# Moving a batched V group ahead of attention, and copying the first context in two halves

## The chip, the core and the metric

The kernel runs on one core of a Trainium2 chip. The metric is the device time of one execution in microseconds (us). The engines are TensorE (PE, with its weight loads as PEld), VectorE (DVE), ScalarE (ACT), GpSimd (POOL) and the DMA queues, the one of SyncE (SP) above all. PSUM, where matmuls leave their results, has eight banks; the text calls them by number.

## The reference

Two blocks follow each other. The first is attention with a recurrent memory: 2048 rows of 512 are cut into 64 segments of 32; in each, 8 memory rows are put ahead, and the first 8 output rows are the next segment's memory. So the segments are a chain.

```python
h = jnp.concatenate([mem, xs], axis=1)              # 8 + 32 rows
q, k, v = (jnp.einsum('btd,dhe->bhte', h, W) for W in (Wq, Wk, Wv))   # 32 heads of 128
scores = jnp.einsum('bhqe,bhke->bhqk', q, k) * scale
p = softmax(where(mask, scores, -1e9))
o = jnp.einsum('bhqk,bhke->bhqe', p, v)
o = jnp.einsum('bhte,hed->btd', o, Wo)
mem = o[:, :M, :]
outs.append(o[:, M:, :])
```

The second is a gMLP: `z = gelu(x @ w_in)`, the second half of z is normalised and mixed over all 2048 positions by `w_sp`, and the product with the first half goes through `w_out`. Both blocks have a layer norm ahead and a residual.

## The kernel before, in words

Every operation is recorded in program order with the tokens that it reads and writes; the recorder derives the semaphore waits, and each engine executes its own list in that order. There is no scheduler: the order of work is the order of the calls.

The loop over s runs through the 64 segments. A segment's 8 memory rows and 24 of its own rows form one stationary operand of 32 columns (`hT`); the last 8 rows of all segments of a chunk of 16 are computed in batches beforehand (`hTe`, "extra" rows). TensorE is used as four column tiles of 128x32 for the projections. The 32 heads are split into two halves b = 0, 1, and in each half into four c = 0 to 3 and four g = 0 to 3.

In a segment TensorE does, in this order: Q and K projections (`QK`, L533), scores (`S_half`, L584 and L590), the V projection (`V_half`, L639) with the softmax sums (`sm_sums`, L605 and L610) between its parts, one batched group of four steps popped from the list `gx`, then attention times V, then the output projection. The popped group is four times four matmuls: Q or K of a later chunk's extra rows (`qkx_mm`, L422) or their V (`vx_mm`, L472), and from segment 49 on part of the second block's first projection (`zp_mm`, L789). Segment 48 has none.

Attention times V is `PV_half(s, b)` for b = 0 and 1: 16 matmuls of 40 columns (L659) with K = 32, in four row tiles of 32x128, one for each c, and 4 matmuls (L666) for the extra rows. The four contexts c go into banks 6, 7, 0 and 1 (`PVB`), half b in columns 160 b to 160 b + 160. L659 of half b reads the normalised weights `E_sb` (DVE, L625) and V (`V_evac`, for b = 1 by DVE L651 and ACT L649), L666 reads the extra rows' weights (GpSimd, L629) and `Vx`, loaded by DMA. The last matmul of half 0's 16 also waits for both copies of half 1's V.

Behind it stands the list `gv`: further batched V groups (and, from segment 49, `zp_mm` groups) in bank 5 (`VXB`), cut into steps of four matmuls. `gv.pour(n)` issues up to n steps and stops when a group is complete, then returning its copy. Its n is `nC`: 3 in segments 0 to 3, 2 in each later segment with s % 4 = 1, else 1. From segment 4 on 8 (or 4, the others later) matmuls of the previous block of rows follow (`WoX_mm`, L738).

Then the four contexts are copied from PSUM to `cT`, each 128x320: c = 0 and 1 by ACT (L679), c = 2 and 3 by DVE (L681). The output projection `Wo` (L693) takes the contexts in the order 0, 2, 1, 3, eight matmuls of 256 columns each, first for output columns 0 to 256 in bank `OB` = 2, then for the rest in bank `OB2` = 0. ACT copies each half of the output into `part` (L705), a few small matmuls pick the memory rows (`mem_out`, L713), ACT puts them into the next segment's `hT` (L716), and the next segment's Q projection starts. Bank 2 also holds the V of half 1 and a piece of K; bank 6 also holds a piece of Q and softmax sums.

After the segments the second block runs, with its own loops.

Of the kernel before, what the change touches and what calls it, by code (L numbers as in the profile page):

```python
# [9 lines left out]
ACT = mybir.ActivationFunctionType  # L10
# [159 lines left out]
def fast_path(nc, st, keep, A_x, A_mem0, A_Wq, A_Wk, A_Wv, A_Wo, A_seg_len, B_w_in, B_w_sp, B_b_sp, B_w_out, out):  # L170
# [17 lines left out]
    scale = float(DH) ** -0.5  # L188
# [74 lines left out]
    ps = st.enter_context(nc.psum_tensor("f_ps", [128, 8, 512], F32))  # L263
# [5 lines left out]
    def PB(b):  # L269
        return ("ps", b)  # L270
# [147 lines left out]
    def qkx_mm(ck, mi, sg, b, bank, dc):  # L418
        ws = (w_q, w_k)[mi]
        for c in range(4):  # L420
            rhs = ws[:, dc, :].rearrange("p (h c i) -> p c h i", c=4, i=32)[:, c, 16 * b:16 * b + 16, :]
            pe(lambda e, c=c, rhs=rhs: e.matmul(ps[32 * c:32 * c + 32, bank, :], lhsT=hTe[:, ck, dc, 32 * sg:32 * sg + 32], rhs=rhs,  # L422
                                                start=(dc == 0), stop=(dc == DC - 1), tile_position=(0, 32 * c)),
               reads=[("hTe", ck), ("W", mi, 2 * b), ("W", mi, 2 * b + 1)], writes=[PB(bank)])

    def qkx_evac(ck, mi, sg, b, bank):
        tok = [("T", 0, 0), ("T", 0, 1)]
        act(lambda e: e.activation(out=Tst[:, 0, :].rearrange("p (hp i r) -> p hp i r", i=32, r=2),
                                   in_=ps[:, bank, :].rearrange("p (hp r i) -> p hp i r", r=2, i=32), func=ACT.Copy),
            reads=[PB(bank)], writes=tok)  # L430
        xi = Tst[:, 0, :].bitcast(U32)
        if mi == 0:
            xt = QTx[ck % 2][:, 0, sg, 8 * b:8 * b + 8, :, :].rearrange("p hp k r -> p (hp k r)").bitcast(U32)
        else:
            xt = KTu[ck % 2][:, 4 * b:4 * b + 4, :, 4 * sg:4 * sg + 4, :]
            xi = xi.rearrange("p (cb hp j k) -> p cb hp j k", j=4, hp=2, k=8)
        dve(lambda e: e.transpose(out=xt, in_=xi), reads=tok, writes=[("QTx", ck % 2, mi, sg, b)])
# [123 lines left out]
    def s_place(s, b):  # L561
        return SBK[b] if s == 0 or b else XB

# [80 lines left out]
    def V_evac(b, eng, gs=(0, 4), after=()):  # L644
# [5 lines left out]
        else:  # L650
            dve(lambda e: e.tensor_scalar(out=dst, in0=src, scalar1=VSC, scalar2=None, op0=ALU.mult), reads=[PB(bank)], writes=tok)  # L651

    def PV_half(s, b):
        xb = s % NVX
        for g in range(4):
            for c in range(4):
                q = slice(32 * c, 32 * c + 32)
                c0 = 160 * b + 40 * g
                pe(lambda e, q=q, c=c, g=g, c0=c0: e.matmul(  # L659
                    ps[:, PVB[c], c0:c0 + 40], lhsT=V_sb[q, b, g * 128:(g + 1) * 128], rhs=E_sb[q, b, 0:160].rearrange("p (a g t) -> p a g t", a=5, t=8)[:, :, g, :],  # L660
                    start=(g == 0), stop=False, skip_group_check=True, tile_position=(32 * c, 0)),
                    reads=[("V", b, g), ("E", b)], writes=[PB(PVB[c])],
                    after=[em.last_w[("V", 1, g)] for g in (0, 2)] if (b, g, c) == (0, 3, 3) else [])
        for c in range(4):
            q = slice(32 * c, 32 * c + 32)
            pe(lambda e, q=q, c=c: e.matmul(  # L666
                ps[:, PVB[c], 160 * b:160 * b + 160].rearrange("p (g q) -> p g q", q=40)[:, :, 0:16], lhsT=Vx[q, xb, b, :],
                rhs=E_sb[q, b, 160:224].rearrange("p (g q) -> p g q", q=16),
                start=False, stop=True, skip_group_check=True, tile_position=(32 * c, 0)),
                reads=[("Vx", xb), ("Ex", b)], writes=[PB(PVB[c])])  # L670

    UNSC = math.exp(-RBIAS)


    def cT_evac(c, eng):
        src = ps[:, PVB[c], 0:320]
        dst = cT[:, c, :]
        if eng == "act":
            act(lambda e: e.activation(out=dst, in_=src, func=ACT.Copy, scale=UNSC), reads=[PB(PVB[c])], writes=[("cT", c)])  # L679
        else:  # L680
            dve(lambda e: e.tensor_scalar(out=dst, in0=src, scalar1=UNSC, scalar2=None, op0=ALU.mult),  # L681
                reads=[PB(PVB[c])], writes=[("cT", c)])

    cTh = cT[:].rearrange("p c (b g q) -> p (c b g) q", b=2, q=40)


    def Wo(cs, bank, d0, d1):
        for c in cs:
            for bg in range(8):
                b, g = bg // 4, bg % 4  # L690
                h = 16 * b + 4 * c + g
                i = 8 * c + bg
                pe(lambda e, h=h, g=g, i=i, b=b, c=c: e.matmul(  # L693
                    ps[32 * g:32 * g + 32, bank, 0:d1 - d0], lhsT=cTh[:, i, 8:40], rhs=w_o[:, h, d0:d1], start=(c == 0 and b == 0),
                    stop=(c == 3 and b == 1), tile_position=(0, 32 * g)),
                    reads=[("cT", c), ("Wo", h // 8)], writes=[PB(bank)])

    def cTx_copy(s):
        j = s % 4
        dst = cTx[:, (s // 4) % 2, :, 8 * j:8 * j + 8]  # L700
        pool(lambda e: e.tensor_copy(out=dst, in_=cTh[:, :, 0:8]), reads=[("cT", c) for c in range(4)],
             writes=[("cTx", (s // 4) % 2)])

    def part_evac(s, bank, d0, d1):
# [29 lines left out]
    def WoX_mm(rb, qr, bgs=range(8)):  # L734
        for bg in bgs:
            b, g = bg // 4, bg % 4
            h = 16 * b + 4 * qr + g
            pe(lambda e, h=h, g=g, i=8 * qr + bg: e.matmul(ps[32 * g:32 * g + 32, WXB, :], lhsT=cTx[:, rb % 2, i, :], rhs=w_o[:, h, :],  # L738
                                                           start=(i < 4), stop=(i >= H - 4), tile_position=(0, 32 * g)),
               reads=[("cTx", rb % 2), ("Wo", h // 8)], writes=[PB(WXB)])  # L740
# [213 lines left out]
    def nC(s, rb, j4):  # L954
        if rb == 0:
            return 3
        return 2 if j4 == 1 else 1
# [9 lines left out]
    for s in range(NSEG):  # L967
        j4 = s % 4
        rb = s // 4
# [78 lines left out]
        xs = gx.pop(0) if gx else []  # L1048
        if s > 3 * CK and zcol:
            zr, zh = zcol.pop(0)  # L1050
            xs = [lambda dc=dc: zp_mm(zr, zh, XB, (dc,)) for dc in range(DC)] + [lambda: zp_evac(zr, zh, XB, "dve")]
        for f in xs[:4]:
            f()
        PV_half(s, 0)
        PV_half(s, 1)
        for f in xs[4:4]:
            f()
        late = []
        if s == 3 * CK + 1:
            for r, hf in zgap:  # L1060
# [13 lines left out]
        cT_evac(3, "dve")  # L1074
# [135 lines left out]
    def zbank():  # L1210
        zcnt[0] += 1
        return 5 + zcnt[0] % 3
# [26 lines left out]
    for i, rb in enumerate(order):  # L1239
# [3 lines left out]
        if i == 0:  # L1243
            F_group(RB - 1, XB)
            for qr in range(4):
# [10 lines left out]
        if i == 1:  # L1256
            WoX_scatter(RB - 1, XB)
            h_done(RB - 1, XB)
# [4 lines left out]
        if i in (3, 4):  # L1263
            r, j, bank = RB - 5 + i, i % 2, zbank()
# [822 lines left out]
```

## Time and profile before

| what | value |
|---|---|
| timed runs | 852.3, 853.75, 855.52 us; median 853.75 |
| the profiled execution's own time | 850.57 us |
| its span in the profile | 847.7 us |
| mean granted TensorE clock | 0.999 |
| the segments, from the first attention matmul of segment 0 to the last segment's | 50.5 to 681.8 us |

The profile shows one execution. A group's row has busy time and mean duration; in brackets, or behind the last bar, stands how long the engine had been idle and what released it. The timeline lists merged runs of equal instructions with their start and the time until the last of them ends. A matmul's duration contains its latency through the array, so matmuls that follow each other overlap in the rows; the chain of waits lists the pieces without this overlap, with the time from one to the next.

### The profile page before, as it was taken

The numbers are of one execution on the slowest core, as the hardware profiler recorded it, in microseconds if no ns is written. First come the engines' busy times: TensorE is split into PE (matmuls) and PEld (weight loads), VectorE is DVE, ScalarE is ACT, GpSimd is POOL, SyncE is SP. The second block draws the span as 40 slices with busy tenths as digits, with TensorE's granted clock in tenths as the row PEclk, the third lists the DMA queues.
The fourth block names the chain that finished last, engine by engine and source line by source line (L and its number), as shares of the span: only waits on it lengthen the run. The fifth ranks groups of instructions, "written<-read, shape, count | busy, mean of one in ns | idle before, by whom it ended". The sixth has DMA issues, their size and how long they took to land.

```text
span 847.7 us, 47962 instructions
## 1 busy us (share of the span) xinstructions
PE 833.5 (98%) x22028; PEld 486.8 (57%) x22034; DVE 493.5 (58%) x1175; ACT 494.0 (58%) x1355; POOL 155.1 (18%) x409
## 2 busy tenths in 40 slices
PE   8999999999999999999999999999999999999997
PEld 8666566656665565656655555556655644444443
DVE  4446566666665656665656666566656577553343
ACT  3456677676777777667777777666666676300000
POOL 5212111112211111121112111112211123100000
PEclk9999999999999999999999999999999999999999
DMA  9972222120201231232213021433332389033101
GB/s 330 385 225 78 70 46 62 51 78 20 82 29 44 63 73 42 66 56 53 69 38 79 30 77 52 83 76 71 70 84 57 71 276 298 1 99 98 46 13 47
DMA packets 95360, 76.04 MB, mean 90 GB/s; under 512 B 46184, under 2 KB 80624, under 8 KB 95152
## 3 DMA queue, kind: packets, MB, share of 16 engines
q1 hardware_dynamic: 93232, 70.09, 28.9%
q8 instruction: 174, 2.85, 1.4%
q10 hardware_dynamic: 1648, 2.49, 0.8%
q0 software_dynamic: 272, 0.33, 0.1%
q14 instruction: 34, 0.28, 0.1%
HBM read 41.75 MB, written 20.91 MB: 74 GB/s over the span
## 4 chain that ended last, share of the span: by engine, by line
PE 94%; DMA 2%; SPq 2%; DVE 1%; issue 0%; ACT 0%; POOL 0%
PE f_ps L533 27%; PE f_ps L693 14%; PE f_ps L639 13%; PE f_ps L1197 11%; PE f_ps L422 4%; PE f_ps L738 3%; PE f_ps L659 3%; PE f_ps L472 3%; PE f_ps L1292 3%; PE f_ps L1190 2%; PE f_ps L789 2%; PE f_ps L445 2%; DMA f_arena<-in_A_Wo_dram 1%; PE f_ps L584 1%; SPq L876 1%; PE f_ps L1157 1%
## 5 line engine op out<-in xcount | busy, mean ns | idle before, releaser
L533 PE MATMUL f_ps<-f_arena,f_hT 128*32 128x512 bf16 (+1 forms) x5120 | 240.9, 337 | 0.4 <-issue 0.3
L533 PEld LDWEIGHTS f_ps<-f_arena,f_hT 128*32 128x32 bf16 x5120 | 117.6, 96 | 98.3 <-ACT f_hT L716 34.4
L544 ACT ACTIVATE f_Tst<-f_ps 128x512 bf16<-128x512 f32 (+2 forms) x320 | 146.8, 511 | 32.7 <-PE f_ps L533 32.0
L639 PE MATMUL f_ps<-f_arena,f_hT 128*32 128x512 bf16 x2048 | 138.8, 379 | 0.0
L693 PE MATMUL f_ps<-f_arena,f_cT 128*32 128x256 bf16 x4096 | 128.1, 272 | 0.5 <-ACT f_cT L679 0.2
L629 POOL TENSOR_TENSOR f_E_sb<-f_R_sb,f_E_sb 128x64 bf16<-128x64 f32 x128 | 47.3, 369 | 390.3 <-ACT f_R_sb L621 389.7
L693 PEld LDWEIGHTS f_ps<-f_arena,f_cT 128*32 128x32 bf16 x4096 | 101.0, 96 | 21.4 <-ACT f_cT L679 18.2
L651 DVE TENSOR_SCALAR f_V_sb<-f_ps 128x512 bf16<-128x512 f32 (+1 forms) x128 | 71.4, 558 | 54.4 <-PE f_ps L639 54.4
L1197 PE MATMUL f_ps<-f_arena 128*128 128x512 bf16 x448 | 100.6, 379 | 0.0
L552 DVE STREAM_TRANSPOSE f_QT<-f_Tst 128x256 uint32<-128x256 uint32 x128 | 57.1, 446 | 65.6 <-ACT f_Tst L544 60.9
L681 DVE TENSOR_SCALAR f_cT<-f_ps 128x320 bf16<-128x320 f32 x128 | 56.8, 486 | 34.2 <-PE f_ps L666 34.2
L1197 PEld LDWEIGHTS f_ps<-f_arena 128*128 128x128 bf16 x448 | 43.7, 98 | 52.6 <-issue 0.2
L705 ACT ACTIVATE f_part<-f_ps 128x256 bf16<-128x256 f32 x128 | 49.2, 384 | 40.6 <-PE f_ps L693 38.4
L598 ACT ACTIVATE f_E_sb<-f_ps 128x224 bf16<-128x224 f32 x128 | 45.4, 355 | 39.2 <-PE f_ps L610 38.6
L679 ACT ACTIVATE f_cT<-f_ps 128x320 bf16<-128x320 f32 x128 | 49.1, 435 | 32.8 <-PE f_ps L666 32.7
L552 DVE STREAM_TRANSPOSE f_KT<-f_Tst 128x256 uint32<-128x256 uint32 (+2 forms) x192 | 60.8, 342 | 5.7 <-ACT f_Tst L544 3.0
L639 PEld LDWEIGHTS f_ps<-f_arena,f_hT 128*32 128x32 bf16 x2048 | 46.0, 95 | 20.0
L716 ACT ACTIVATE f_hT<-f_ps 128x16 bf16<-128x16 f32 x126 | 23.2, 184 | 46.3 <-PE f_ps L713 46.3
L570 DVE CAST f_ps<-f_mask 128x224 f32<-128x224 bf16 x80 | 29.8, 373 | 35.0 <-ACT f_hT L402 32.0
L1203 DVE TENSOR_TENSOR f_arena<-f_ps,f_arena 128x512 f32<-128x512 f32 x28 | 19.3, 689 | 52.7 <-PE f_ps L1197 52.7
L621 ACT ACTIVATE f_R_sb<-f_R_sb 128x160 f32<-128x160 f32 x128 | 43.1, 337 | 4.4 <-ACT f_Vs L484 0.4
L422 PE MATMUL f_ps<-f_arena,f_hTe 128*32 128x512 bf16 x640 | 41.5, 379 | 0.0
(128 smaller groups left out, 1153.2 us busy)
## 6 DMA issues: line engine op xcount, KB each, us to landing
wT_d<-f_wst SPq DMA_DIRECT2D x32, 256.0 KB, 2.6
f_arena<-wT_d SPq DMA_DIRECT2D x32, 256.0 KB, 5.5
f_arena<-in_A_Wv_dram SPq DMA_DIRECT2D x4, 1024.0 KB, 14.0
f_arena<-in_A_Wk_dram SPq DMA_DIRECT2D x4, 1024.0 KB, 14.6
f_arena<-in_A_Wo_dram SPq DMA_DIRECT2D x4, 1024.0 KB, 12.2
f_Vx<-vext_d SPq DMA_DIRECT2D x62, 64.0 KB
vext_d<-f_Vs SPq DMA_DIRECT2D x22, 128.0 KB, 2.9
zp_d<-f_Vs SPq DMA_DIRECT2D x20, 112.0 KB, 1.6
```

The source lines that it names most:

```text
L422: pe(lambda e, c=c, rhs=rhs: e.matmul(ps[32 * c:32 * c + 32, bank, :], lhsT=hTe[:, ck, dc, 32 * sg:32 * sg + 32], rhs=rhs, start=(dc == 0) ...
L533: pe(lambda e, dc=dc, c=c, rhs=rhs: e.matmul(ps[32 * c:32 * c + 32, bank, 0:32 * nh], lhsT=hT[:, sl, dc, :], rhs=rhs, start=(dc == 0), sto ...
L544: act(lambda e: e.activation(out=st_.rearrange("p (hp i r) -> p hp i r", i=32, r=2), in_=ps[:, bank, 0:64 * np_].rearrange("p (hp r i) -> ...
L552: dve(lambda e: e.transpose(out=dst, in_=src), reads=tok, writes=[(nm, b, k) for k in halves(b, p0, np_)])
L629: pool(lambda e: e.tensor_tensor(out=ev, in0=rv, in1=ev, op=ALU.mult), reads=[("R", b), ("Ex", b)], writes=[("Ex", b)])
L639: pe(lambda e, dc=dc, c=c, c0=c0: e.matmul(ps[32 * c:32 * c + 32, bank, 0:w], lhsT=hT[:, sl, dc, :], rhs=w_v[:, dc, c0:c0 + w], start=(dc ...
L651: dve(lambda e: e.tensor_scalar(out=dst, in0=src, scalar1=VSC, scalar2=None, op0=ALU.mult), reads=[PB(bank)], writes=tok)
L679: act(lambda e: e.activation(out=dst, in_=src, func=ACT.Copy, scale=UNSC), reads=[PB(PVB[c])], writes=[("cT", c)])
L681: dve(lambda e: e.tensor_scalar(out=dst, in0=src, scalar1=UNSC, scalar2=None, op0=ALU.mult), reads=[PB(PVB[c])], writes=[("cT", c)])
L693: pe(lambda e, h=h, g=g, i=i, b=b, c=c: e.matmul(ps[32 * g:32 * g + 32, bank, 0:d1 - d0], lhsT=cTh[:, i, 8:40], rhs=w_o[:, h, d0:d1], star ...
L705: act(lambda e: e.activation(out=part[:, s % 8, d0:d1], in_=ps[:, bank, 0:d1 - d0], func=ACT.Copy), reads=[PB(bank)], writes=[("part", s % ...
L1197: pe(lambda e: e.matmul(ps[:, bank, 0:TB], lhsT=z2[:, sc, fb * 128:(fb + 1) * 128], rhs=wTb[tb % 2][:, :, sc, :], start=first, stop=last), ...
```

## The change

The banks: `OB` becomes 6, and a new constant `CB` = 2 is the bank of context 0 in half 1, by `pv_bank(b, c)`. The first context so lies in two banks: half 0 in bank 6 columns 0 to 160, half 1 in bank 2 columns 160 to 320. In half 1 the 16 matmuls of a `PV_half` go through the contexts in the order 1, 2, 3, 0. The wait of half 0's last matmul for half 1's V is gone; half 1's matmuls wait for it themselves.

The copy of context 0 becomes two ACT copies of 128x160: one between the two halves of attention in the program, one where the whole copy stood. The token `("cT", c)` is split by half, so that `Wo` waits for what each matmul reads.

The order: one step of `gv` is issued ahead of `PV_half(s, 0)`; what remains of `nC` follows behind attention, unless the first step completed a group.

```diff
-    OB = 2
+    OB = 6
     XB = 3
+    CB = 2
...
+    PVO = ((0, 1, 2, 3), (1, 2, 3, 0))
+
+    def pv_bank(b, c):
+        return CB if (b, c) == (1, 0) else PVB[c]
...
-            for c in range(4):
+            for c in PVO[b]:
...
-                    reads=[("V", b, g), ("E", b)], writes=[PB(PVB[c])],
-                    after=[em.last_w[("V", 1, g)] for g in (0, 2)] if (b, g, c) == (0, 3, 3) else [])
+                    reads=[("V", b, g), ("E", b)], writes=[PB(pv_bank(b, c))])
...
-    def cT_evac(c, eng):
-        src = ps[:, PVB[c], 0:320]
-        dst = cT[:, c, :]
+    def cT_evac(c, eng, b=None):
+        bank = pv_bank(b, c)
+        cols = slice(0, 320) if b is None else slice(160 * b, 160 * b + 160)
+        src = ps[:, bank, cols]
+        dst = cT[:, c, cols]
+        tok = [("cT", c, k) for k in ((0, 1) if b is None else (b,))]
...
-                    reads=[("cT", c), ("Wo", h // 8)], writes=[PB(bank)])
+                    reads=[("cT", c, b), ("Wo", h // 8)], writes=[PB(bank)])
...
-        PV_half(s, 0)
-        PV_half(s, 1)
-        for f in xs[4:4]:
-            f()
         late = []
...
-        pv = gv.pour(nC(s, rb, j4))
+        pv = gv.pour(1) if nC(s, rb, j4) else []
+        PV_half(s, 0)
+        cT_evac(0, "act", 0)
+        PV_half(s, 1)
+        if not pv:
+            pv = gv.pour(nC(s, rb, j4) - 1)
...
-        cT_evac(0, "act")
+        cT_evac(0, "act", 1)
         cT_evac(2, "dve")
         cT_evac(1, "act")
         cT_evac(3, "dve")
```

More of the change, by code (lines that the diff above doesn't have):

```diff
@@ L659, in PV_half @@
                 pe(lambda e, q=q, c=c, g=g, c0=c0: e.matmul(
-                    ps[:, PVB[c], c0:c0 + 40], lhsT=V_sb[q, b, g * 128:(g + 1) * 128], rhs=E_sb[q, b, 0:160].rearrange("p (a g t) -> p a g t", a=5, t=8)[:, :, g, :],
+                    ps[:, pv_bank(b, c), c0:c0 + 40], lhsT=V_sb[q, b, g * 128:(g + 1) * 128], rhs=E_sb[q, b, 0:160].rearrange("p (a g t) -> p a g t", a=5, t=8)[:, :, g, :],
                     start=(g == 0), stop=False, skip_group_check=True, tile_position=(32 * c, 0)),
-                    reads=[("V", b, g), ("E", b)], writes=[PB(PVB[c])],
@@ L663, in PV_half @@
-                    after=[em.last_w[("V", 1, g)] for g in (0, 2)] if (b, g, c) == (0, 3, 3) else [])
-        for c in range(4):
+                    reads=[("V", b, g), ("E", b)], writes=[PB(pv_bank(b, c))])
+        for c in PVO[0]:
             q = slice(32 * c, 32 * c + 32)
             pe(lambda e, q=q, c=c: e.matmul(
-                ps[:, PVB[c], 160 * b:160 * b + 160].rearrange("p (g q) -> p g q", q=40)[:, :, 0:16], lhsT=Vx[q, xb, b, :],
+                ps[:, pv_bank(b, c), 160 * b:160 * b + 160].rearrange("p (g q) -> p g q", q=40)[:, :, 0:16], lhsT=Vx[q, xb, b, :],
@@ L668, in PV_half @@
                 rhs=E_sb[q, b, 160:224].rearrange("p (g q) -> p g q", q=16),
                 start=False, stop=True, skip_group_check=True, tile_position=(32 * c, 0)),
-                reads=[("Vx", xb), ("Ex", b)], writes=[PB(PVB[c])])
+                reads=[("Vx", xb), ("Ex", b)], writes=[PB(pv_bank(b, c))])
     UNSC = math.exp(-RBIAS)
-    def cT_evac(c, eng):
-        src = ps[:, PVB[c], 0:320]
-        dst = cT[:, c, :]
+    def cT_evac(c, eng, b=None):
[4 more added lines that the diff above has]
+        tok = [("cT", c, k) for k in ((0, 1) if b is None else (b,))]
@@ L678, in cT_evac @@
         if eng == "act":
-            act(lambda e: e.activation(out=dst, in_=src, func=ACT.Copy, scale=UNSC), reads=[PB(PVB[c])], writes=[("cT", c)])
+            act(lambda e: e.activation(out=dst, in_=src, func=ACT.Copy, scale=UNSC), reads=[PB(bank)], writes=tok)
         else:
             dve(lambda e: e.tensor_scalar(out=dst, in0=src, scalar1=UNSC, scalar2=None, op0=ALU.mult),
-                reads=[PB(PVB[c])], writes=[("cT", c)])
+                reads=[PB(bank)], writes=tok)
     cTh = cT[:].rearrange("p c (b g q) -> p (c b g) q", b=2, q=40)
@@ L700, in cTx_copy @@
         dst = cTx[:, (s // 4) % 2, :, 8 * j:8 * j + 8]
-        pool(lambda e: e.tensor_copy(out=dst, in_=cTh[:, :, 0:8]), reads=[("cT", c) for c in range(4)],
+        pool(lambda e: e.tensor_copy(out=dst, in_=cTh[:, :, 0:8]), reads=[("cT", c, b) for c in range(4) for b in range(2)],
              writes=[("cTx", (s // 4) % 2)])
```

## The prediction

> **What bounds the kernel now.** I read the page's head and its chain first, then the timeline of single segments, because the change sits in one place that every one of the 64 segments passes.
>
> ```profile
> span 847.7 us, 47962 instructions
> PE 833.5 (98%) x22028; PEld 486.8 (57%) x22034; DVE 493.5 (58%) x1175; ACT 494.0 (58%) x1355; POOL 155.1 (18%) x409
> ...
> PE 94%; DMA 2%; SPq 2%; DVE 1%; issue 0%; ACT 0%; POOL 0%
> ```
>
> The chain that ends last is TensorE's for 94% of the span. But a matmul's row includes its way through the array, so "98% busy" still hides short stretches in which nothing enters. They must be read from starts. Below is the seam of an ordinary segment (batched Q/K group L422, attention L659 and L666, batched V group L472, memory projection L738, output projection L693) in the timeline: start, duration, engine, line. A sixteen-matmul group, and four matmuls of 512 columns, take what the chain of waits says behind it.
>
> ```profile
> 301.02 0.35 PE L659 MATMUL f_ps<-f_E_sb,f_V_sb 32*128 32x40 bf16 x16
> ...
> 310.01 1.04 PE L422 MATMUL f_ps<-f_arena,f_hTe 128*32 128x512 bf16 x16
> ...
> 310.58 0.55 DVE L625 TENSOR_TENSOR f_E_sb<-f_R_sb,f_E_sb 128x160 bf16<-128x160 f32 x2
> 310.70 0.38 ACT L649 ACTIVATE f_V_sb<-f_ps 128x256 bf16<-128x256 f32 x1
> 310.87 0.43 POOL L629 TENSOR_TENSOR f_E_sb<-f_R_sb,f_E_sb 128x64 bf16<-128x64 f32 x1 [0.32 <-ACT f_R_sb L621]
> 310.98 0.24 PEld L659 LDWEIGHTS f_ps<-f_E_sb,f_V_sb 32*128 32x128 bf16 x16 [0.42 <-DVE f_E_sb L625]
> 310.98 0.34 PE L659 MATMUL f_ps<-f_E_sb,f_V_sb 32*128 32x40 bf16 x16
> 311.14 0.22 PE L666 MATMUL f_ps<-f_E_sb,f_Vx 32*128 32x64 bf16 x4
> 311.19 0.27 PE L659 MATMUL f_ps<-f_E_sb,f_V_sb 32*128 32x40 bf16 x16
> 311.35 0.21 PE L666 MATMUL f_ps<-f_E_sb,f_Vx 32*128 32x64 bf16 x4
> 311.49 0.40 PE L472 MATMUL f_ps<-f_arena,f_hTe 128*32 128x512 bf16 x4
> 311.58 0.77 ACT L679 ACTIVATE f_cT<-f_ps 128x320 bf16<-128x320 f32 x2 [0.50 <-PE f_ps L666]
> 311.65 0.89 DVE L681 TENSOR_SCALAR f_cT<-f_ps 128x320 bf16<-128x320 f32 x2 [0.52 <-PE f_ps L666]
> 311.71 0.61 PE L738 MATMUL f_ps<-f_arena,f_cTx 128*32 128x512 bf16 x8
> 312.15 1.05 PE L693 MATMUL f_ps<-f_arena,f_cT 128*32 128x256 bf16 x32
> ```
>
> ```profile
> 441.13 0.04 PE f_ps L666 x4
> 441.16 0.10 PE f_ps L659 x16
> ...
> 450.03 0.21 PE f_ps L639 x4
> 450.24 0.86 PE f_ps L422 x16
> ```
>
> Four things are to be seen. (1) L422 has been fed at 310.01 + 0.86 = 310.87, and attention starts at 310.98: 0.10 to 0.11 empty. (2) Attention then takes 310.98 to 311.35 up to its last group (call that start V), 0.37, although its pieces by themselves are 0.10 and 0.04 per half. It is paced from outside: the first L666 comes 0.06 after ACT's V copy ends (310.70 + 0.38 = 311.08), the second L659 0.06 after the second DVE product (310.58 + 0.55 = 311.13), the second L666 0.05 after GpSimd's product (311.30). (3) From V to the next ordinary matmul is 0.14, with no wait named. (4) The output projection starts at V + 0.80. ACT's first context copy is ready before that; the batched V group and L738 cover it.
>
> Where the batched V groups have run out the seam looks different:
>
> ```profile
> 451.04 0.35 PE L659 MATMUL f_ps<-f_E_sb,f_V_sb 32*128 32x40 bf16 x16
> ...
> 451.41 0.21 PE L666 MATMUL f_ps<-f_E_sb,f_Vx 32*128 32x64 bf16 x4
> ...
> 451.55 0.62 PE L738 MATMUL f_ps<-f_arena,f_cTx 128*32 128x512 bf16 x8
> ...
> 452.13 0.89 PEld L693 LDWEIGHTS f_ps<-f_arena,f_cT 128*32 128x32 bf16 x36 [0.47 <-ACT f_cT L679]
> ...
> 460.94 0.34 PE L659 MATMUL f_ps<-f_E_sb,f_V_sb 32*128 32x40 bf16 x16
> ```
>
> L738 is fed at 451.55 + 2 x 0.21 = 451.98, and L693 waits for ACT's copy until 452.13 = V + 0.72. The two seams also tell whether time at this point is time of the kernel. The V group's 0.21 moves L693 by 0.80 - 0.72 = 0.08, and the segment with it lasts 9.96 (301.02 to 310.98) against 9.90 (451.04 to 460.94): 0.06 of 0.08 arrives in the period. So a gain at the first L693 is passed on nearly whole.
>
> In the last quarter the work before attention is L789:
>
> ```profile
> 550.50 0.93 PE L789 MATMUL f_ps<-f_arena 128*32 128x448 bf16 x16
> ...
> 551.07 0.55 DVE L625 TENSOR_TENSOR f_E_sb<-f_R_sb,f_E_sb 128x160 bf16<-128x160 f32 x2
> ...
> 551.36 0.42 POOL L629 TENSOR_TENSOR f_E_sb<-f_R_sb,f_E_sb 128x64 bf16<-128x64 f32 x1 [0.32 <-ACT f_R_sb L621]
> 551.44 0.38 PE L659 MATMUL f_ps<-f_E_sb,f_V_sb 32*128 32x40 bf16 x16
> ...
> 551.84 0.21 PE L666 MATMUL f_ps<-f_E_sb,f_Vx 32*128 32x64 bf16 x4
> 551.98 0.37 PE L789 MATMUL f_ps<-f_arena 128*32 128x448 bf16 x4
> ...
> 552.61 0.61 PE L693 MATMUL f_ps<-f_arena,f_cT 128*32 128x256 bf16 x16
> ```
>
> Sixteen of these are fed in about 0.76 (448/512 of 0.86), until 551.26; attention waits for DVE's first product and starts 0.18 later. L693 follows at V + 0.77.
>
> **The change, part by part.** *Kinds of segments.* Counted through the program's order, 38 segments (0 to 2, 4 to 38) have both an ordinary group before attention and V groups: kind A. Ten (39 to 47 and 63) have no V group: B. Fourteen (49 to 62) have L789 before and after: C, where four (every fourth) put two pieces there. Segments 3 and 48 I leave at nothing.
>
> *One group of four matmuls moved ahead of attention.* It costs 0.21 before attention (0.19 in C) and saves as much behind; nothing is added. In A attention starts 0.21 later, if the empty 0.10 stays. By then all three outside paces are past (the latest, 311.35, is 0.37 after the old start; the new second L666 is due at 0.21 + 0.24 = 0.45), so attention shrinks to its own 0.14 + 0.10, with 0.01 for the first loads 0.25. V moves by 0.21 + 0.25 - 0.37 = +0.09 to 0.10. In C attention starts 0.19 + 0.10 - 0.18 = 0.11 later; GpSimd's product still ends at 551.78 and releases the last group at 551.84, so V doesn't move.
>
> *What becomes late next.* Behind V there is now only L738, fed until V + 0.14 + 0.43 = V + 0.57 (in B that is so already). The first copy's left half is taken from bank 6 in the middle of attention, which the second half no longer writes (its first context goes to bank 2, free since the V copies). The right half is taken 0.23 after V, as the whole copy is now (311.58). Its length:
>
> ```profile
> L679 ACT ACTIVATE f_cT<-f_ps 128x320 bf16<-128x320 f32 x128 | 49.1, 435 | 32.8 <-PE f_ps L666 32.7
> ...
> L649 ACT ACTIVATE f_V_sb<-f_ps 128x256 bf16<-128x256 f32 x64 | 24.6, 384 | 0.8 <-DVE f_V_sb L651 0.8
> ...
> L544 ACT ACTIVATE f_Tst<-f_ps 128x192 bf16<-128x192 f32 x64 | 20.9, 327 | 0.0
> ...
> L681 DVE TENSOR_SCALAR f_cT<-f_ps 128x320 bf16<-128x320 f32 x128 | 56.8, 486 | 34.2 <-PE f_ps L666 34.2
> ```
>
> From 435, 384 and 327 ns for 320, 256 and 192 columns, 160 columns should take 300 ns. Two copies of 435 end after 0.77 (the 311.58 row), so a successor starts 0.10 before the end of the one ahead. Left half: V + 0.09 to V + 0.39 in A. Right half: V + 0.29 to V + 0.59, ready for TensorE 0.06 later at V + 0.65; L693 needs it after four left-half matmuls, at V + 0.57 + 0.11 = V + 0.68. ACT's second context follows from V + 0.49 to V + 0.92. The DVE copy isn't touched: 311.65 + 0.49 = V + 0.79, ready at V + 0.85. L693 wants it second, at V + 0.57 + 0.21 = V + 0.78. So the wait moves from ACT's first copy to DVE's first, which sets the second context's start at V + 0.85 in all three kinds. ACT's second is wanted at V + 1.06 and is there at V + 0.98; DVE's second (0.89 after 311.65, V + 1.19) is wanted at V + 1.27. The extra ACT work, 0.2 per segment once overlap is taken off, falls where ACT waits for TensorE anyway (32.8 us of idle before L679); nothing else stands in its queue between the V copy and these copies. The copies behind end about 0.03 later than now in A and earlier in B.
>
> *Sum.* The second context's start was V + 0.80 + 0.21 = V + 1.01 in A, V + 0.93 in B, V + 0.98 in C (V + 0.95 where two pieces stood). A: 1.01 - 0.85 - 0.10 = 0.06, times 38 = 2.3. B: 0.93 - 0.85 = 0.08, times 10 = 0.8. C: 0.13 times 10 and 0.10 times 4 = 1.7. Together 4.8 us.
>
> *Edits at nothing.* The bank 6 for the first output sum: its copy ends before the next segment's Q projection writes bank 6, since the memory rows that stand ahead of that projection read the same copy. If that cover failed, it would be a part of one 0.38 copy per segment. Bank 2 is likewise read out before the next K piece comes. The wait for the V copies moves from the end of attention's first half into its second; it holds the same later matmuls and in A and C is past. The order 1, 2, 3, 0 in the second half changes no count.
>
> [...] The row with two copies in 0.77 says neighbours overlap by 0.10. [...]
>
> *The rule on the empty 0.10.* DVE's first product alone:
>
> ```profile
> 310.58 0.32 DVE L625 TENSOR_TENSOR f_E_sb<-f_R_sb,f_E_sb 128x160 bf16<-128x160 f32 x1
> ```
>
> The profile puts the gap before L659 down to DVE. But that product ends at 310.90, and 0.06 after that is 310.96, not 310.98; and the same 0.10 stands behind attention with no wait at all (V's group of 0.04, then 0.14 to the next start). I take it as the price of changing between 128x32 and 32x128 tiles, which stays. [...]
>
> **The rivals.** *The gap was only DVE's wait.* Then in A attention starts 0.11 after its old start, V stays within 0.01, and A gains 0.15 to 0.16 per segment: 38 x 0.16 + 2.5 = 8.6 us. For it: the named releaser. Against it: the equal gap behind.
>
> *Attention keeps its 0.37.* If its pace is its own, V moves by 0.21 in A and 0.11 in C: A loses 0.05 (38 x 0.05 = 1.9), B gains 0.8, C 0.02 x 10 = 0.2: 0.9 us slower, within what can be told. Against it: the three hand-offs of 0.05 to 0.06.
>
> *Slower: ACT's three copies queue end to end.* Then in A they end at V + 0.39, 0.69 and 1.12, ready at V + 1.18 where L693 wants the second at 1.06. The third context, formerly due at V + 1.22, then stands at V + 1.18 + 0.10: 38 x 0.06 = 2.3 lost; B still gains 0.7, C 0.3. Result 1.3 us slower. It decides once ACT's second context is ready after V + 1.12. Against it: the 0.77 row.
>
> *No effect by a return of the wait.* The gain could be taken back at the copies of L705 behind L693. The 9.96 against 9.90 speaks against it.
>
> **How the numbers follow.** The profiled execution took 850.57 us at a span of 847.7; it is below the median of the three timed runs, 853.75 (852.3 to 855.52). 850.57 - 4.8 = 845.8; carried to the median, 849.0. The rivals stand at 845.2, 854.7 and 855.0, no effect at 853.75. Chances: forecast 0.60, gap closing 0.12, attention's own pace 0.10, ACT queue 0.08, handed back 0.10. Half a per cent, 4.3 us, is about what a measurement here can tell; my forecast lies just over it, so with runs scattering by a few us some 0.6 of its chance counts as faster (0.36) and the rest as same; with the gap's 0.12 that is 0.48. Slower by over half a per cent needs two rivals at once, or something unseen: 0.06. The rest, 0.46, is same. Range 845.0 to 855.0.
>
> **What would show it.** Right: L659 still starts 0.10 after the moved group is fed; attention up to V takes 0.25 in A; L693 starts at about V + 0.57 and waits for L681 (DVE), not L679 (ACT); 160-column copies near 300 ns; segments in A last 9.90, in C 0.13 less than now. Wrong: an L693 wait named ACT, attention of 0.37, or segments as long as now though L693 starts earlier.

## The result, and the profile after

| kernel | median, us | runs | ratio to before, 95% interval |
|---|---|---|---|
| before | 853.52 | 22 | |
| changed | 851.72 | 22 | 0.9975 [0.9964, 0.9986] |

The change is faster by 0.25%, 2.1 us (1.2 to 3.1). The time lies in the forecast range and is lower, as forecast; but 4.8 us was forecast, more than twice what came.

About 1.0 of these 2.1 us lies outside the program's span, the time from its first instruction to its last. The 22 executions of the changed kernel take 1.66 to 1.85 us longer than their spans. The profiled execution of before takes 2.83 us longer (850.57 against 847.74), and its executions beside the experiments 2.56 to 3.12. So about 1 us is gained inside the span. The prediction speaks of the segments alone.

The page of the changed kernel's profiled execution, head and chain:

```profile
span 847.7 us, 48032 instructions
PE 832.2 (98%) x22034; PEld 475.2 (56%) x22034; DVE 493.3 (58%) x1175; ACT 498.4 (59%) x1419; POOL 154.8 (18%) x409
...
PE 93%; DMA 3%; SPq 2%; issue 1%; ACT 0%; DVE 0%; POOL 0%; POOLq 0%
```

Its span is that of before, 847.7, and its own time of 849.45 us is 1.1 below the 850.57 of before's. So this execution shows the part of the gain outside the span and none inside; where that went is told below. The segments do show a gain. The same seam as in the prediction, kind A, in the timeline of the changed kernel (L665 and L671 are attention, L687 ACT's and L689 DVE's copies, L746 the memory projection, L701 the output projection):

```profile
291.24 1.04 PE L422 MATMUL f_ps<-f_arena,f_hTe 128*32 128x512 bf16 x16
...
291.81 0.55 DVE L626 TENSOR_TENSOR f_E_sb<-f_R_sb,f_E_sb 128x160 bf16<-128x160 f32 x2
...
292.10 0.39 PE L472 MATMUL f_ps<-f_arena,f_hTe 128*32 128x512 bf16 x4
...
292.42 0.27 PE L665 MATMUL f_ps<-f_E_sb,f_V_sb 32*128 32x40 bf16 x16
...
292.53 0.20 PE L671 MATMUL f_ps<-f_E_sb,f_Vx 32*128 32x64 bf16 x4
...
292.56 0.28 PE L665 MATMUL f_ps<-f_E_sb,f_V_sb 32*128 32x40 bf16 x16
...
292.68 0.21 PE L671 MATMUL f_ps<-f_E_sb,f_Vx 32*128 32x64 bf16 x4
292.78 0.83 ACT L687 ACTIVATE f_cT<-f_ps 128x160 bf16<-128x160 f32 x3 [0.47 <-PE f_ps L671]
...
292.82 0.62 PE L746 MATMUL f_ps<-f_arena,f_cTx 128*32 128x512 bf16 x8
293.04 0.89 DVE L689 TENSOR_SCALAR f_cT<-f_ps 128x320 bf16<-128x320 f32 x2 [0.68 <-PE f_ps L671]
...
293.58 0.50 PEld L701 LDWEIGHTS f_ps<-f_arena,f_cT 128*32 128x32 bf16 x20 [0.15 <-DVE f_cT L689]
...
302.39 0.27 PE L665 MATMUL f_ps<-f_E_sb,f_V_sb 32*128 32x40 bf16 x16
```

The moved group is fed until 292.10 + 0.21 = 292.31 and attention starts 0.11 later. Attention's last group starts at V = 292.68, 0.26 after the first. The first wait of the output projection that holds TensorE is the one for DVE's copy. All that is as forecast. But DVE's copy starts at V + 0.36, where 0.30 was forecast, and the segment lasts 9.97 (292.42 to 302.39): not shorter than before.

Kinds B and C, where attention and the next segment's attention start, and the wait for DVE's copy:

```profile
483.58 0.27 PE L665 MATMUL f_ps<-f_E_sb,f_V_sb 32*128 32x40 bf16 x16
...
484.79 0.23 PEld L701 LDWEIGHTS f_ps<-f_arena,f_cT 128*32 128x32 bf16 x12 [0.15 <-DVE f_cT L689]
...
493.38 0.27 PE L665 MATMUL f_ps<-f_E_sb,f_V_sb 32*128 32x40 bf16 x16
```

```profile
573.29 0.27 PE L665 MATMUL f_ps<-f_E_sb,f_V_sb 32*128 32x40 bf16 x16
...
573.91 0.89 DVE L689 TENSOR_SCALAR f_cT<-f_ps 128x320 bf16<-128x320 f32 x2 [0.56 <-PE f_ps L671]
...
583.13 0.27 PE L665 MATMUL f_ps<-f_E_sb,f_V_sb 32*128 32x40 bf16 x16
```

B lasts 9.80 (9.90 before), C 9.84 (9.93 before). Over all undisturbed segments the medians change by +0.007 in A, by -0.09 in B, and in C by -0.10, or by -0.07 in the four with two pieces (9.90 before): 38 x 0.007 - 10 x 0.09 - 10 x 0.10 - 4 x 0.07 = -1.9 us. That this comes close to the 2.1 us measured is partly luck: inside the span only about 1 us of it arrived.

### The profile page after: what moved, and what is told of

It is laid out like the page before. It is cut to its first block, busy times and chain, and to the rows that moved or that the text cites. A ratio compares the mean times of both kernels' runs of the same rounds, so it can differ in the third digit from the quotient of the medians.

```text
span 847.7 us, 48032 instructions
## 1 busy us (share of the span) xinstructions
PE 832.2 (98%) x22034; PEld 475.2 (56%) x22034; DVE 493.3 (58%) x1175; ACT 498.4 (59%) x1419; POOL 154.8 (18%) x409
## 3 DMA queue, kind: packets, MB, share of 16 engines
q8 instruction: 174, 2.85, 1.5%
## 4 chain that ended last, share of the span: by engine, by line
PE 93%; DMA 3%; SPq 2%; issue 1%; ACT 0%; DVE 0%; POOL 0%; POOLq 0%
PE f_ps L534 27%; PE f_ps L701 14%; PE f_ps L640 13%; PE f_ps L1206 11%; PE f_ps L422 4%; PE f_ps L746 4%; PE f_ps L1301 3%; PE f_ps L472 3%; PE f_ps L665 2%; PE f_ps L797 2%; PE f_ps L1199 2%; PE f_ps L445 2%; DMA f_arena<-in_A_Wo_dram 1%; PE f_ps L585 1%; SPq L884 1%; PE f_ps L606 1%
## 5 line engine op out<-in xcount | busy, mean ns | idle before, releaser
L701 PE MATMUL f_ps<-f_arena,f_cT 128*32 128x256 bf16 x4096 | 134.6, 273 | 1.2 <-issue 0.5
L701 PEld LDWEIGHTS f_ps<-f_arena,f_cT 128*32 128x32 bf16 x4096 | 95.8, 95 | 31.8 <-ACT f_cT L687 8.8
L689 DVE TENSOR_SCALAR f_cT<-f_ps 128x320 bf16<-128x320 f32 x128 | 56.8, 486 | 40.7 <-PE f_ps L671 40.7
L687 ACT ACTIVATE f_cT<-f_ps 128x160 bf16<-128x160 f32 (+1 forms) x192 | 53.8, 346 | 26.5 <-PE f_ps L671 26.5
L746 PE MATMUL f_ps<-f_arena,f_cTx 128*32 128x512 bf16 x512 | 41.5, 383 | 0.0
```

Of the source, the lines that this page charges most:

```text
L701: pe(lambda e, h=h, g=g, i=i, b=b, c=c: e.matmul(ps[32 * g:32 * g + 32, bank, 0:d1 - d0], lhsT=cTh[:, i, 8:40], rhs=w_o[:, h, d0:d1], star ...
```

## Experiments

Periods are read from attention's start to the next, in segments without the stops told of below. All ratios are to the kernel before, with runs on the same chip. The experiments ran on four chips in all, so times of two experiments can differ by some tenths of a us for that alone (before's median is 853.1 to 853.9).

| run | time, us | ratio, 95% interval | A, B, C period, us |
|---|---|---|---|
| before | 853.52 | | 9.96, 9.90, 9.93 |
| changed | 851.72 | 0.9975 [0.9964, 0.9986] | 9.97, 9.81, 9.84 |
| split only | 853.46 | 1.0002 [0.9986, 1.0018] | 9.96, 9.80, 9.93 |
| move only | 856.71 | 1.0033 [1.0015, 1.0051] | 10.03, 9.89, 9.90 |
| short copy of context 2 | 847.48 | 0.9936 [0.9917, 0.9956] | 9.85, 9.74, 9.74 |
| copies rebalanced | 848.96 | 0.9951 [0.9933, 0.9969] | 9.91, 9.74, 9.78 |
| half step | 853.28 | 0.9996 [0.9977, 1.0015] | 9.86, 9.80, 9.83 |
| half step, rebalanced | 854.33 | 1.0012 [0.9995, 1.0029] | 9.86, 9.75, 9.78 |
| less attention (one run) | 846.8 | | 9.90, 9.80, 9.81 |
| half step, whole copy | 855.66 | 1.0031 [1.0012, 1.0050] | 9.93, 9.90, 9.90 |
| split steps only | 857.93 | 1.0055 [1.0031, 1.0079] | 9.96, 9.89, 9.93 |
| before, no transposes | 851.11 | 0.9965 [0.9952, 0.9979] | 9.95, 9.90, 9.92 |
| changed, no transposes | 847.12 | 0.9937 [0.9922, 0.9953] | 9.97, 9.81, 9.83 |
| half step, no transposes | 847.50 | 0.9932 [0.9915, 0.9949] | 9.86, 9.80, 9.83 |

**Split only and move only: the two parts of the change.**

```diff
 split only (on the changed kernel)
-        pv = gv.pour(1) if nC(s, rb, j4) else []
         PV_half(s, 0); cT_evac(0, "act", 0); PV_half(s, 1)
-        if not pv:
-            pv = gv.pour(nC(s, rb, j4) - 1)
+        pv = gv.pour(nC(s, rb, j4))
 move only (on the kernel before)
+        pv = gv.pour(1) if nC(s, rb, j4) else []
         PV_half(s, 0); PV_half(s, 1)
-        pv = gv.pour(nC(s, rb, j4))
+        if not pv:
+            pv = gv.pour(nC(s, rb, j4) - 1)
```

> The first context is split over two banks and copied in two halves, but all batched V groups stay behind attention. Theory (the changed kernel's gain ends where DVE's copy of context 2 becomes the wait of the output projection): with the V group behind attention that copy is covered, so kind A (a V group in the segment) stays at 9.96 us per segment and kind C at 9.93; kind B (none) gains the 0.09 that it gains in the full change, together 0.9 us faster than before. Rival (the second ACT copy itself costs time, and that ate kind A's gain): kind A gets longer, about 0.05 per segment, 1 us or more slower in all.

> One V step goes ahead of attention, the first context stays whole in one bank and is copied whole, output sum in bank 2 as before. Theory: attention's last group starts 0.10 us later in kind A, and the whole copy of context 0 (ready about V + 0.76) becomes the wait of the output projection, so that context 2 starts at V + 0.98: kind A loses 0.06 to 0.08 per segment, B nothing, C about 0; 2 to 3 us slower than before. Rival (the split is what costs, the move alone is a gain): kind A gains up to 0.05 per segment, 2 us or more faster.

The periods come as the theory has them: the split alone gains B's 0.09 and costs A nothing; its 0.9 us is within the interval of the time, so the time itself is inconclusive, but the rival's loss in A is excluded. The move alone costs A 0.07 and the whole 2.8 us. So neither part gains by itself what both gain; in A the split pays back what the move costs.

The two also tell what delays DVE's copy. A segment of the move alone, with the old banks and the old order of contexts:

```profile
255.12 0.27 PE L659 MATMUL f_ps<-f_E_sb,f_V_sb 32*128 32x40 bf16 x16
...
255.36 0.22 PE L666 MATMUL f_ps<-f_E_sb,f_Vx 32*128 32x64 bf16 x4
...
255.71 0.49 DVE L681 TENSOR_SCALAR f_cT<-f_ps 128x320 bf16<-128x320 f32 x1 [0.66 <-PE f_ps L666]
```

The copy starts at V + 0.35 here, 0.59 after attention's start, while in the split alone, with the new banks and order but attention held from outside as before, the median is V + 0.30. So in A most of the delay comes with attention that isn't held. The rest, 0.62 in place of 0.59 after attention's start, comes with the new banks and order.

**Short copy of context 2: is DVE's copy the wait?**

```diff
-        cT_evac(2, "dve")
+        cT_evac(2, "dve", 0 if s else None)
```

> The changed kernel, but from the second segment on DVE copies only the left 160 columns of context 2; the right 160 columns of that context are left as they were in the first segment. Theory: DVE's copy of context 2 ends about 0.17 us earlier, TensorE finds contexts 2, 1 and 3 ready, and the third context starts at V + 1.02 in place of V + 1.14: kinds A and C shorten by 0.11 per segment, B by 0.06, together 6 us faster than the changed kernel (about 8 us faster than before). Rival (kind A's gain is returned at a later wait, so a segment cannot get shorter here): segments as long as in the changed kernel, though the output projection starts its second context earlier.

The timeline of kind A:

```profile
290.34 0.21 PE L671 MATMUL f_ps<-f_E_sb,f_Vx 32*128 32x64 bf16 x4
...
290.70 0.72 DVE L689 TENSOR_SCALAR f_cT<-f_ps 128x160 bf16<-128x160 f32 x2 [0.68 <-PE f_ps L671]
...
290.80 0.79 PEld L701 LDWEIGHTS f_ps<-f_arena,f_cT 128*32 128x32 bf16 x28 [0.19 <-ACT f_cT L687]
```

The copy still starts at V + 0.36, but the weight loads of the output projection now run on without a DVE wait, and A falls by 0.12, B by 0.07, C by 0.09. That DVE's copy of context 2 held the changed kernel is shown, and the periods come as forecast. The time is 0.64% below before's, 5.5 us where 8 was forecast, and 4.2 us below the changed kernel's median, where 6 was.

**Copies rebalanced: a version that beats both.**

```diff
-        cT_evac(0, "act", 1); cT_evac(2, "dve"); cT_evac(1, "act"); cT_evac(3, "dve")
+        cT_evac(0, "dve", 1); cT_evac(1, "act"); cT_evac(2, "dve"); cT_evac(3, "act")
-        Wo((0, 2, 1, 3), OB, 0, OC)   # and (0, 2, 1) for the second sum
+        Wo((0, 1, 2, 3), OB, 0, OC)   # and (0, 1, 2)
```

> The changed kernel with the copies dealt out anew: DVE takes the right half of context 0 and then context 2, ACT takes contexts 1 and 3, and the output projection goes 0, 1, 2, 3. Theory: context 1 by ACT ready at V + 0.79, wanted at V + 0.80; context 2 by DVE ready at V + 1.08, so the third context starts at V + 1.08 in place of V + 1.14: kinds A and C 0.05 shorter, B about as in the changed kernel; 2.5 us faster than the changed kernel, 4.5 us faster than before. Rival (gain returned later): as the changed kernel.

A 9.91, B 9.74, C 9.78, and 0.9951: the forecast of 4.5 us against before is met (4.2). It is the fastest kernel here that computes all.

**Half a step ahead of attention, and less attention: what A lost.**

```diff
 half step: every V step as 2 x 4 matmuls of 256 columns; the left ones ahead
+            m((0,))
         PV_half(s, 0); cT_evac(0, "act", 0); PV_half(s, 1)
+            m((1,))
 less attention
-        for g in range(4):
+        for g in range(3):
```

> The changed kernel, but of the V step ahead of attention only the left 256 columns go ahead; the right 256 follow behind attention (every batched V step is issued as two times four matmuls of 256 columns). The second block's steps (from segment 49 on) stay whole. Theory (kind A gained nothing because a whole step pushes attention 0.10 past the end of its outside pace, so that the copies come later): half a step, 0.11, fits into that pace, V stays where it was, the output projection starts at V + 0.69 with all copies in time; kind A goes from 9.97 to 9.85 per segment, B and C as in the changed kernel, 4.3 us faster than the changed kernel, 6.4 us faster than before. Rival (kind A cannot gain here, whatever stands ahead of attention): kind A stays at 9.96, as the changed kernel in all.

> The changed kernel, with the fourth of the four matmul groups of each half of attention left out (8 of 40 matmuls per segment; those parts of the contexts are not computed). Theory: in kinds A and C of the changed kernel attention runs at TensorE's own pace, so 2 x 0.025 us go out of each segment: 9.92 and 9.78; in B it is paced by GpSimd's product and stays at 9.81. Rival (attention is paced from outside in A and C too): no segment gets shorter.

Two attention starts of the half step, and two of less attention, kind A:

```profile
323.46 0.27 PE L673 MATMUL f_ps<-f_E_sb,f_V_sb 32*128 32x40 bf16 x16
...
333.32 0.27 PE L673 MATMUL f_ps<-f_E_sb,f_V_sb 32*128 32x40 bf16 x16
```

```profile
250.90 0.25 PE L665 MATMUL f_ps<-f_E_sb,f_V_sb 32*128 32x40 bf16 x12
...
260.80 0.25 PE L665 MATMUL f_ps<-f_E_sb,f_V_sb 32*128 32x40 bf16 x12
```

With half a step A lasts 9.86, 0.10 less than before, with V where it was: A can gain, and a whole step is too much. With fewer attention matmuls A gets shorter by 0.07 and C by 0.03, B not at all. In A the last group now starts 0.19 after attention's start in place of 0.26: attention there runs at TensorE's own pace. In C that distance stays 0.29, held from outside as the prediction has it; only DVE's copy comes 0.03 earlier. But the half step's time, 853.28, is that of before; 6.0 us of shorter segments (38 x 0.10 + 10 x 0.09 + 14 x 0.09) are missing, and inside the span a little more, since about 1 us is gained outside it here too. The two companions say the same:

> The half step of the run before together with the copies dealt out anew (DVE: right half of context 0, context 2; ACT: contexts 1 and 3; order 0, 1, 2, 3). Theory: A as with the half step alone (9.85, no copy is late there any more), B 9.75 and C 9.78 as with the rebalanced copies; 7.5 us faster than before. Rival: no faster than the rebalanced copies alone.

> Half a V step ahead of attention, but the first context whole in one bank and copied whole, output sum in bank 2, as before the change. Theory: V stays, the output projection waits for the whole copy of context 0 until V + 0.73 and then runs through; kind A gains 0.07 (9.89), B nothing, C 0.03; 3 us faster than before. Rival (without the split copy no gain): 0 or slower.

Both have shorter segments than before (9.86 and 9.93 in A) and no better time, 854.33 and 855.66. The first one's periods were forecast; the second one's A is 9.93 where 9.89 was forecast. Neither time was.

**Where the shorter segments went.** In the half step's timeline:

```profile
155.54 0.39 PE L709 MATMUL f_ps<-f_arena,f_cT 128*32 128x256 bf16 x7
...
156.34 0.27 PE L709 MATMUL f_ps<-f_arena,f_cT 128*32 128x256 bf16 x1 [0.41 <-issue]
156.34 0.26 PEld L392 LDWEIGHTS f_ps<-f_ident,f_xn 128*32 128x32 bf16 x15 [0.69 <-issue]
```

Seven of eight equal matmuls run, then TensorE stands, its queue waiting for nothing that the profile shows ("issue"). Counted through the trace of the changed kernel, such stops stand behind matmuls 10701, 11979, 13513 and 16454: 1278, 1534 and 2941 apart, that is 10, 12 and 23 times 128, but for a few missing records. The page's DMA row for instructions, of the changed kernel:

```profile
q8 instruction: 174, 2.85, 1.5%
```

2.85 MB in 174 packets are 16.4 KB each. The queue brings TensorE's instructions: with 512 matmuls fewer (less attention) it has 170 packets, with 224 more (half step) 176, that is one packet for 128 matmuls and their weight loads. In the changed kernel 22034 matmuls and as many loads over 174 packets make 253 instructions each.

The timing fits too. In the traces of all 20 kernels 196 matmuls in the segments (from 53 us on) start 0.40 us or more after the matmul ahead. In 152 of the 196 a packet of this queue had ended 1.2 to 1.6 us earlier, though such packets come only every 3.9 us or so; in the half step it is 14 of 15. So at most of these stops TensorE goes on 1.2 to 1.6 us after its instruction packet has come. The theory for the next runs was: TensorE stops at the end of an instruction block when the next has not come. Four runs:

```diff
 split steps only: the kernel before with V steps of 2 x 4 matmuls, nothing moved
 no transposes: before, changed, half step
-        if s % 2 == 1 and s // 2 < NWT:
-            wT_piece(s // 2)
```

> The kernel before, in which only the batched V steps are issued as two times four matmuls of 256 columns in place of four of 512: 224 matmuls and their weight loads more, the same columns, nothing moved. Theory (TensorE's instructions come in blocks of 128 matmuls with their weight loads, and TensorE stops for 0.3 to 0.7 us at block ends where the next is not there yet): segments of kind A stay at 9.96 where no such stop falls, but stops get more or longer; 1 to 3 us slower than before. Rival (the half step's missing gain lies elsewhere, in what it moves): no change, within 0.5 us.

> The kernel before without the 32 transposing loads of w_sp and the stores behind them in the segments; the second block reads w_sp untransposed with loads of the same size, so its mixing is not the reference's. Theory (the block ends stop because other DMA traffic holds the instruction fetch up, the transposing loads above all): the stops of 0.3 us and more in the segments get fewer, 1 to 4 us faster than before, periods between them unchanged. Rival (fetching is late by itself): the same stops, same time within 1 us.

> The changed kernel without those loads and stores, second block as in the run before. Theory: 2 us faster than the kernel before without them (the segments' own gain), stops as rare there. Rival (the change itself makes stops): less than 1 us faster than that kernel.

> The half-step kernel without those loads and stores. Theory (its 0.10 per segment of kind A was handed back at block ends): without the traffic that delays the fetch it is 4 to 6 us faster than the kernel before without them. Rival (the stops come from the number of instructions alone): no faster than that kernel, with 0.3 to 0.7 us stops at block ends as many as with the transposing loads.

The same columns in 224 more matmuls cost 4.6 us, more than the 1 to 3 expected, with every undisturbed period as before (9.96, 9.89, 9.93). That is most of what the half step lacks, and it lies in the stops: in the traces the segments' excess over their undisturbed periods is 3.3 us in all in before, 7.7 with split steps only and 12.0 in the half step.

Without the transposing loads before gains 2.2 us against the median beside it, the changed kernel stands 4.0 below that (2 was forecast) and the half step 3.6. About 1 us of these two again lies outside the span. So inside it about 2.7 of the half step's 6.0 us show, and "4 to 6" is missed. In the traces the excess falls from 5.5 to 2.1 us in the changed kernel and from 12.0 to 3.4 in the half step; in before it stays 3.3, so the fewer stops forecast there are not shown.

**Number of instructions or place of the block ends?**

```diff
-    for i in range(78):
+    for i in range(78 + 64):      # and + 32, - 32: tiny matmuls at the start
```

> The kernel before with 64 more of the tiny warm-up matmuls (8 columns, about 0.01 us each, 0.6 us, where TensorE still waits for its first data) at the very start, so that every later block end of 128 matmuls falls half a block earlier in the program. Theory (the block ends stop by where they fall against waits and transfers): the time moves by more than 1 us, either way. Rival (only the number of instructions counts): 0 to 0.6 us slower.

> The half-step kernel with the same 64 tiny matmuls at the start. Theory (its loss came from where its 224 more matmuls put the block ends): 2 us or more off the half-step kernel's time, to 851 or 855. Rival (only the number counts): 0 to 0.6 us slower than the half-step kernel.

> The kernel with the rebalanced copies and the same 64 tiny matmuls. Theory: moves by more than 1 us against 849.0 of the rebalanced copies. Rival: 0 to 0.6 us slower than those.

> The rebalanced copies with 32 more tiny matmuls at the start: block ends a quarter of a block earlier in the program. Theory (where the block ends fall decides 2 to 5 us): a time between 849 and 853, not equal to either by need. Rival (a shift costs by its length): 851.

> The rebalanced copies with 32 tiny matmuls fewer at the start, block ends a quarter of a block later. Theory: a time between 847 and 853. Rival (a shift costs by its length, fewer is a gain): 848.5, 0.3 us of tiny matmuls less than 849.0.

> Half step and rebalanced copies with 32 more tiny matmuls: 224 + 32 are two whole blocks, so that from the segment on in which the V steps end all block ends fall as in the rebalanced kernel. Theory: the second half of the segments loses no more at block ends than there; 2 to 4 us faster than the half step with rebalanced copies without the shift, 850 to 852. Rival (number alone): 0.3 us slower than that kernel.

| kernel | tiny matmuls | time, us | ratio, 95% interval |
|---|---|---|---|
| before | +64 | 857.74 | 1.0052 [1.0035, 1.0070] |
| half step | +64 | 855.24 | 1.0026 [1.0011, 1.0041] |
| rebalanced | +64 | 853.06 | 1.0011 [0.9994, 1.0028] |
| rebalanced | +32 | 849.64 | 0.9968 [0.9948, 0.9988] |
| rebalanced | -32 | 850.20 | 0.9976 [0.9955, 0.9997] |
| half step, rebalanced | +32 | 851.14 | 0.9978 [0.9961, 0.9994] |

Weight loads of the output projection in the list of waits, before, before with 64 more tiny matmuls, and the half step (total, times, longest):

```profile
PEld f_ps L693 <- issue: 0.2, 1, 0.2
```

```profile
PEld f_ps L693 <- issue: 2.6, 3, 1.7
```

```profile
PEld f_ps L709 <- issue: 4.9, 11, 0.8
```

Half a block's shift costs before 4.7 us and the rebalanced kernel 4.1, for 64 matmuls of about 0.01 us; periods between stops don't move (9.96, 9.89, 9.93 in before). To a quarter of a block either way the rebalanced kernel is slower by 0.7 and 1.2, within the intervals, which settles nothing. With 224 + 32 = two blocks the half step with rebalanced copies gains 3.2 us over itself unshifted and is faster than before, though its number is greater. So the place of the block ends counts: half a block's shift cost about twice what the change gained. The half step moved by 2.0 under the half block's shift, as far as forecast.

In the traces 2.5 and 2.9 us of the shifted kernels' loss fall in segment 0: it lasts 13.07 us in before with 64 more tiny matmuls (10.62 in before) and 13.31 in the rebalanced kernel with them (10.46 without). The stop in the first of these, and what came behind it (stretches, each engine's busy time, granted clock, DMA share and GB/s):

```profile
52.94 0.62 PE L472 MATMUL f_ps<-f_arena,f_hTe 128*32 128x512 bf16 x4 [0.99 <-issue]
```

```profile
49.20:52.80 3.60, 1.71 (x56) 0.76 (x49) 1.54 (x4) 1.72 (x6) 1.56 (x4) 1.00 1.02 338
52.80:56.20 3.40, 3.26 (x60) 2.74 (x63) 0.69 (x1) 0.38 (x1) 0.05 (x1) 0.50 0.36 115
```

The stop falls where the DMA engines are busy all the time (share 1.02), and behind it the granted clock of TensorE is 0.50 for 3.4 us. The rebalanced kernel's trace with 64 more has the same, at 53.8 us. So the segment with the stop of 0.99 us lost more than that, 2.5 us. What makes an instruction packet late is not settled: other DMA traffic is a candidate, and without the transposing loads the excess is 3.4 us smaller in the changed kernel (5.5 to 2.1) and 8.6 in the half step (12.0 to 3.4).

The 1 us outside the span may be of the same kind. In all six kernels with the output sum in bank 2 as before, one more instruction packet of 8 KB (queue q14) starts 2.5 to 2.9 us after the program's last instruction; in the 14 with the changed banks none does. The changed kernel and the half step have 64 more ACT instructions than before (1419 against 1355); that this is the reason is not shown.

## Why the prediction was right or wrong

- *The gap before attention* stayed at 0.10 to 0.11 with the moved group ahead, though DVE's first product had ended at 291.81 + 0.32 = 292.13, 0.29 before attention's start. The first rival, that the gap is DVE's wait, is out. That the 0.10 is the price of changing between 128x32 and 32x128 tiles was the author's estimate; no run separates it from other causes.
- *Attention* shrank from 0.37 to 0.26 in A (forecast 0.25). V moved by 0.10, as forecast (0.58 after the end of L422's feeding in place of 0.48). The second rival is out.
- *The copies of 160 columns* took 302 ns (forecast 300):

```profile
L687 ACT ACTIVATE f_cT<-f_ps 128x160 bf16<-128x160 f32 x128 | 32.8, 302 | 26.5 <-PE f_ps L671 26.5
```

  Three copies of 302, 302 and 435 ended within 0.83, so each overlaps the one ahead by 0.10. From 302 and 435 the fixed part of a copy is about 0.17 (an estimate: 302 less the 133 for 160 columns more), so some 0.07 of it stays in each added copy. Splitting cost ACT no more than was summed, and the rival of the queueing copies is out.
- *The step that failed* is "ready at V + 0.85" in kind A: DVE's copy was taken to start 0.30 after V, as in the kernel before. There V was held up by GpSimd (V 0.05 after its product's end). With attention at its own pace (0.26 to V in place of 0.37) DVE's copy starts at V + 0.36. Context 2 then started at V + 0.91, not 0.85, and context 1 another 0.01 late. Against 1.01 - 0.10 that is nothing: A's term of 2.3 us came out as -0.3.
- Two things make up this 0.06. The larger is attention's pace: the move alone, with old banks and order, has the copy at V + 0.35, and with less attention it comes 0.07 earlier after attention's start. The smaller is the new banks and order, of which the prediction says that they change "no count": the copy starts 0.62 after attention's start in A and in C alike with them, and 0.59 in both without (move only, and half step with whole copy). Which of banks, order and the moved wait for V does it, no run separates.
- *C* had the same term smaller (V + 0.33; 0.31 in move only, so here it came with the banks and order): 0.10 for 0.13, and 0.07 for 0.10 where two pieces stood, 1.3 us for 1.7. *B*, with attention held as before, came as forecast: 0.09 for 0.08.
- The sum with these sizes is 0.9 + 1.3 - 0.3 = 1.9. The gain in an undisturbed segment is passed on, as the prediction read from 9.96 and 9.90: the short copy's context 1 came 0.12 earlier, and the period with it.
- What the prediction left out are the stops at block ends and the time outside the span. In the profiled executions the segments' excess over the undisturbed periods is 5.5 us in all, against 3.3 in before, which is why the span didn't fall. In the medians about half of the 1.9 us is lost inside the span, and the 1.0 us outside it makes up for that. So the total comes near the segments' sum partly by luck.

## What to carry to other kernels

Here work moved ahead of a step that is held from outside was free up to the slack in that holding: half a V step (half of 0.21 us) left V where it was and made A 0.10 shorter. Beyond it, with a whole step, V came 0.10 later, attention ran at its own pace (0.26 to V in place of 0.37), and the start times read while it was held no longer told when its results come (DVE's copy at V + 0.36 in place of 0.30). When a wait goes, size the next one from the producer's own start, not from the consumer's distance in the old trace. And where shorter periods don't reach the total, count where the engine stands "waiting for nothing": in this long unrolled program half a block's shift of the instruction blocks' ends was worth more (4.7 us in before) than the edit (2.1). Compare the time with the span as well: here half of the gain lay outside it.

## What the runs showed of the hardware

TensorE stopped for 0.3 to 0.7 us, at times over 1 us, and the stops counted in the changed kernel stand behind matmul numbers 10, 12 and 23 times 128 apart, but for a few missing records; packets of 16.4 KB, 174 for 22034 matmuls, 176 with 224 more and 170 with 512 fewer, bring its instructions. Of 196 gaps of 0.40 us or more between matmul starts in the traces of all 20 kernels, 152 ended 1.2 to 1.6 us after such a packet. Behind the stops in segment 0 of before and of the rebalanced kernel, each with 64 more tiny matmuls, the granted clock was 0.50 for 3.4 us. These 64, about 0.6 us in all (an estimate: before's 78 take 0.71, from 1.09 to the next matmul at 1.80), moved the whole of before by 4.7 us, 224 matmuls that add no columns by 4.6 us, and the absence of 32 transposing loads with their stores by 2.2 us (0.9965). The time outside the span was 1.7 to 1.9 us with the changed banks and 2.4 to 3.1 with the old ones, where one more instruction packet came 2.5 to 2.9 us after the last instruction.
